# Weight preparation in a fused depthwise and pointwise convolution: copies as four concurrent 32-row matmuls, and the weight rows loaded by parity

## The chip, the cores and the metric

The kernel runs on one core of a Trainium2 chip. The metric is the time of one execution on the device in microseconds (us). Medians are given with the lowest and highest run. A profile is one execution; its "span" runs from the first to the last instruction, and is some 1.7 us shorter than the time of the same execution.

## The reference

A depthwise convolution with a 1x1 kernel is a scaling of each channel; a pointwise one is a matrix product. With H = W = C = D = 384 and bf16 throughout:

```python
def reference(x, dw, pw):            # x (1,384,384,384), dw (1,1,384), pw (384,384)
    out = x * dw[0, 0]               # k = 1: no padding, no sum over taps
    return jnp.einsum('bhwc,cd->bhwd', out, pw)
```

The kernel folds dw into pw, w[c, d] = dw[c] * pw[c, d], and multiplies 147456 pixels by w.

## The kernel before

Pixels are worked through in 288 "supertiles" of 512. VectorE transposes 32x32 blocks of channel pairs (bf16 pairs as one 32-bit word), so the channels of a 64-channel block b stand as pairs on 32 partitions. A matmul then takes the even or the odd channel of each pair (`par`), 32 rows deep, four of them side by side on the four 32-row strips of the array:

```python
mm = nc.tensor.matmul(PS[s][:, q, :D],                      # the main loop, 48 per supertile
        lhsT=Ts[s][32*q : 32*q+32, b, par::2],
        rhs=w_r[32*q : 32*q+32, b, par, :],
        tile_position=(32*q, 0), ...)
```

Each strip q needs the same 32 weight rows of (b, par), so w_r holds every row four times over the partitions. That is prepared once, in the "head", ahead of the loop. pw is loaded in natural order, 128 rows outermost. A 0/1 selector, scaled by dw, picks 32 rows and copies them to four strips in one 128-row matmul; ScalarE and VectorE then move the result out of PSUM:

```python
nc.sync.dma_start(pw_n[:, 0, :], pw[:P, :]).then_inc(s_pw[0], 16)
nc.sync.dma_start(pw_n[:, 1:3, :], pw[P:, :].rearrange("(k p) d -> p k d", p=P)).then_inc(s_pw[1], 16)
# ... TensorE:
idle_work(4)                          # rounds of four matmuls of zeros
# dw on partitions: 3 matmuls of 128 columns;  then idle_work(2)
for b in range(NB):                   # NB = 6
    # ... waits for pw, the scaled selector, PSUM banks that are free again
    for r in range(2):
        mm = nc.tensor.matmul(w_ps(b)[:, r, :], lhsT=sel_w[:, b//2, 2*(b%2)+r, :],
                              rhs=pw_n[:, b//2, :], start=True, stop=True)
    mm.then_inc(s_w)
# six evictions of 128x768: number 1 on VectorE, the other five on ScalarE
```

## Time and profile before

| | before |
|---|---|
| time, median of 6 (lowest to highest) | 576.05 us (575.57 to 578.58) |
| span of the profiled run | 573.9 us |
| first main matmul | 7.40 us |
| 288 supertiles | 561.8 us, 1.951 us each |
| after the start of the last group of matmuls | 5.1 us |

TensorE sets the time. From 7.40 us it never waits, so the time is the head, plus 288 x 1.951 us, plus the last eviction and store. The prediction shows the lines. A group of four concurrent matmuls of 384 columns takes 0.1625 us in the loop, and twice as long, 0.32 us, while the array runs at half rate. In the lines of the profile, PE is TensorE's matmuls and PEld its weight loads, DVE is VectorE, ACT ScalarE, POOL GpSimd and SP SyncE; a q behind the name stands for the queue that issues that engine's DMAs, L is a line of the kernel, and x with a number is a count.

### The profile page before, as it was taken

Reading aid. Unit: us, or ns where it says so; the run is one execution under the profiler, and the core shown is the slowest. Engines: PE = TensorE matmul, PEld = TensorE weight load, DVE = VectorE, ACT = ScalarE, POOL = GpSimd, SP = SyncE. Lnnn points to the kernel's source line nnn. Section 1 sums busy time; section 2 is a strip of 40 time slices with the busy share of each in tenths; the row PEclk is TensorE's granted clock in tenths of the full one; section 3 lists DMA queues with packets and bytes.
Section 4 is the critical chain, followed back from the end, with each engine's and each line's share of the span. In section 5 each row is a group of like instructions: output and inputs, shape, how many; then the busy total and the mean of one; then the engine's idle time right before and its main releaser. Section 6 shows DMA issues by size and latency. Waiting matters only on the chain.

```text
span 573.9 us, 29696 instructions
## 1 busy us (share of the span) xinstructions
PE 567.2 (99%) x13863; PEld 412.2 (72%) x13863; DVE 506.9 (88%) x582; ACT 418.9 (73%) x296; POOL 1.7 (0%) x8
## 2 busy tenths in 40 slices
PE   8999999999999999999999999999999999999996
PEld 4777777777777777777777777777777777777774
DVE  6898988988898898889889988988998898899884
ACT  6777777777777777777777777777777777777775
POOL 1000000000000000000000000000000000000000
PEclk9999999999999999999999999999999999999999
DMA  8999999999999999999999999999999999994996
GB/s 339 432 391 427 421 418 426 435 429 417 382 405 420 385 392 436 392 390 397 434 391 385 398 434 383 400 400 432 399 387 422 407 384 398 422 392 156 410 404 244
DMA packets 25928, 226.88 MB, mean 395 GB/s; under 512 B 1213, under 2 KB 5694, under 8 KB 22078
## 3 DMA queue, kind: packets, MB, share of 16 engines
q1 hardware_dynamic: 25916, 226.79, 98.1%
q14 instruction: 9, 0.07, 0.0%
q8 instruction: 1, 0.02, 0.0%
q10 hardware_dynamic: 2, 0.00, 0.0%
HBM read 113.54 MB, written 113.25 MB: 395 GB/s over the span
## 4 chain that ended last, share of the span: by engine, by line
PE 98%; ACT 1%; DMA 0%; DVE 0%; issue 0%; POOL 0%; POOLq 0%; SPq 0%
PE ps L165 97%; PE ps L182 0%; DMA out_dram<-O 0%; PE ps L214 0%; ACT w_r L268 0%; ACT O L296 0%; DVE O L293 0%; POOL zero L229 0%; POOL warm L228 0%; PE ps L197 0%; POOLq L326 0%; SPq L99 0%
## 5 line engine op out<-in xcount | busy, mean ns | idle before, releaser
L165 PE MATMUL ps<-w_r,T 32*128 32x384 bf16 x13824 | 561.8, 321 | 0.5 <-ACT w_r L268 0.5
L255 DVE STREAM_TRANSPOSE T<-X 128x384 uint32<-128x384 uint32 x576 | 504.0, 878 | 55.9 <-DMA X<-in_x_dram 1.2
L296 ACT CAST O<-ps 128x1536 bf16<-128x1536 f32 x288 | 413.6, 1436 | 147.7 <-PE ps L165 147.7
L165 PEld LDWEIGHTS ps<-w_r,T 32*128 32x128 bf16 x13824 | 410.2, 93 | 152.0 <-issue 0.8
L268 ACT CAST w_r<-ps 128x768 bf16<-128x768 f32 x5 | 3.7, 810 | 1.9 <-PE ps L214 1.8
L182 PE MATMUL ps<-zero 32*128 32x384 bf16 x24 | 2.6, 494 | 1.4 <-POOL zero L229 1.4
L293 DVE CAST O<-ps 128x768 bf16<-128x768 f32 x1 | 1.0, 957 | 3.0 <-DMA out_dram<-O 3.0
L273 DVE COPY dw_f<-ps 128x3 f32<-128x3 f32 x1 | 0.2, 160 | 3.3 <-PE ps L197 3.3
L214 PE MATMUL ps<-pw_n,sel_w 128*128 128x384 bf16 x12 | 2.8, 382 | 0.1
L182 PEld LDWEIGHTS ps<-zero 32*128 32x128 bf16 x24 | 0.7, 99 | 2.6 <-issue 2.6
L214 PEld LDWEIGHTS ps<-pw_n,sel_w 128*128 128x128 bf16 x12 | 1.2, 111 | 1.8 <-issue 0.9
L241 ACT ACT_TABLE_LOAD x1 | 1.3, 1283 | 1.5 <-SPq L99 1.5
L268 DVE CAST w_r<-ps 128x768 bf16<-128x768 f32 x1 | 1.0, 958 | 1.0 <-PE ps L214 1.0
L277 DVE TENSOR_SCALAR sel_w<-sel,dw_f 128x512 bf16<-128x512 bf16 x3 | 0.9, 348 | 0.1
L231 POOL TENSOR_SCALAR_AFFINE_SELECT sel<-ones 128x512 bf16<-128x512 bf16 x1 | 0.7, 735 | 0.1
L230 POOL MEMSET ones<- 128x512 bf16 x1 | 0.5, 529 | 0.0
L197 PEld LDWEIGHTS ps<-ones,dw_row 1*128 1x128 bf16 x3 | 0.2, 98 | 0.2 <-issue 0.2
L241 ACT COPY warm<-warm 128x1 f32<-128x1 f32 x2 | 0.3, 189 | 0.0
L229 POOL MEMSET zero<- 128x192 uint32 x1 | 0.3, 258 | 0.0
L197 PE MATMUL ps<-ones,dw_row 1*128 1x1 bf16 x3 | 0.2, 160 | 0.0
L228 POOL MEMSET warm<- 128x3 f32 x1 | 0.1, 101 | 0.5 <-SPq L99 0.5
L315 POOL MEMSET const-bfloat16-1.0<- 128x1 bf16 x1 | 0.1, 101 | 0.0
(3 smaller groups left out, 0.3 us busy)
## 6 DMA issues: line engine op xcount, KB each, us to landing
X<-in_x_dram SPq DMA_DIRECT2D x26, 3840.0 KB, 21.5
out_dram<-O SPq DMA_DIRECT2D x26, 3840.0 KB, 27.4
X<-in_x_dram SPq DMA_DIRECT2D x2, 1536.0 KB, 17.3
out_dram<-O SPq DMA_DIRECT2D x2, 1536.0 KB, 13.3
X<-in_x_dram SPq DMA_DIRECT2D x3, 768.0 KB, 7.5
out_dram<-O SPq DMA_DIRECT2D x3, 768.0 KB, 11.1
X<-in_x_dram SPq DMA_DIRECT2D x1, 2304.0 KB, 19.0
out_dram<-O SPq DMA_DIRECT2D x1, 2304.0 KB, 11.8
```

What stands on the lines that cost most here:

```text
L165: mm = nc.tensor.matmul(PS[s][:, q, :D], lhsT=Ts[s][32 * q : 32 * q + 32, b, par::2], rhs=w_r[32 * q : 32 * q + 32, b, par, :], start=(b = ...
L182: nc.tensor.matmul(PS[0][:, i, :D], lhsT=zero[32 * i : 32 * i + 32, 0:P], rhs=zero[32 * i : 32 * i + 32, :], start=True, stop=True, tile_p ...
L197: mm = nc.tensor.matmul(PS[1][:, k, D : D + 1], lhsT=dw_row[:, P * k : P * k + P], rhs=ones[0:1, 0, 0:1], start=True, stop=True,)
L214: mm = nc.tensor.matmul(w_ps(b)[:, r, :], lhsT=sel_w[:, b // 2, 2 * (b % 2) + r, :], rhs=pw_n[:, b // 2, :], start=True, stop=True,)
L230: nc.gpsimd.memset(ones[:], 1.0).then_inc(s_seed)
L231: nc.gpsimd.affine_select(out=sel[:].rearrange("p (v r) (q w) -> p v r q w", v=2, q=4), in_=ones[:].rearrange("p (v r) (q w) -> p v r q w" ...
L241: c = nc.scalar.copy(warm[:, s + 1 : s + 2], warm[:, 0:1])
L255: ins = nc.vector.transpose(out=Tw[:, 3 * h : 3 * h + 3], in_=Xw[:, :, j, 96 * h : 96 * h + 96].rearrange("p k (b w) -> p b k w", w=32),)
L268: i = nc.vector.tensor_copy(out, in_) if e == 0 else nc.scalar.copy(out, in_)
L277: nc.vector.tensor_scalar_mul(sel_w[:, k], sel[:], dw_f[:, k : k + 1]).then_inc(s_sw)
L293: e = nc.vector.tensor_copy(Ov[:, nq:4, j, :], PS[s][:, nq:4, :D])
L296: a = nc.scalar.copy(Ov[:, 0:nq, j, :], PS[s][:, 0:nq, :D])
```

## The change

The intent is a shorter head. Four weight copies run side by side on the four strips, with one 32-column selector in place of four 128-column ones. Each strip must then hold 32 rows of the same parity, so the load permutes the rows of pw: within each third (128 rows), even rows to partitions 0 to 63, odd ones to 64 to 127. dw is spread by twelve 32-column matmuls, and two idle rounds are dropped. Cut to its core:

```diff
-        nc.sync.dma_start(pw_n[:, 0, :], pw[:P, :]).then_inc(s_pw[0], 16)
-        nc.sync.dma_start(pw_n[:, 1:3, :], pw[P:, :].rearrange("(k p) d -> p k d", p=P)).then_inc(s_pw[1], 16)
+        for k, eng in enumerate((nc.sync, nc.sync, nc.scalar)):
+            rows = pw[P * k : P * k + P, :].rearrange("(u r) d -> r u d", r=2)
+            eng.dma_start(pw_n[:, k, :], rows).then_inc(s_pw[k], 16)
 # [cut: main loop, last four groups in the order (4,0) (5,0) (4,1) (5,1)]
-        idle_work(4)
+        idle_work(3)
 # [cut: dw by twelve matmuls of 32 columns instead of three of 128]
-        idle_work(2)
-        for b in range(NB):
+        idle_work(1)
+        for k in range(3):
 # [cut: waits for pw third k, selector k, and for k == 2 the first two evictions]
+            for j in range(4):
                 mm = nc.tensor.matmul(
-                    w_ps(b)[:, r, :],
-                    lhsT=sel_w[:, b // 2, 2 * (b % 2) + r, :],
-                    rhs=pw_n[:, b // 2, :],
+                    PS[(k + 1) % 2][:, j, :D],
+                    lhsT=sel_w[32 * j : 32 * j + 32, k, :, :].rearrange("p q w -> p (q w)"),
+                    rhs=pw_n[32 * j : 32 * j + 32, k, :],
+                    tile_position=(32 * j, 0),
 # [cut: selector from a 128x128 unit matrix by a VectorE reduction; evictions by parity]
```

More of the change, by code (lines that the diff above doesn't have):

```diff
@@ L67 @@
     pw_n = consts.tile([P, 3, D], BF16, name="pw_n")
-    ones = consts.tile([P, 4, P], BF16, name="ones")
-    sel = consts.tile([P, 4, P], BF16, name="sel")
-    sel_w = consts.tile([P, 3, 4, P], BF16, name="sel_w")
+    ones = consts.tile([P, P], BF16, name="ones")
+    eye = consts.tile([P, P], BF16, name="eye")
+    sel = consts.tile([P, 32], F32, name="sel")
+    sel_w = consts.tile([P, 3, 4, 32], BF16, name="sel_w")
     w_r = consts.tile([P, NB, 2, D], BF16, name="w_r")
@@ L88 @@
     s_dw = nc.alloc_semaphore("s_dw")
-    s_pw = [nc.alloc_semaphore(f"s_pw{h}") for h in range(2)]
+    s_pw = [nc.alloc_semaphore(f"s_pw{h}") for h in range(3)]
     s_df = nc.alloc_semaphore("s_df")
@@ L147 @@
         w_eng = [1, 0, 1, 1, 1, 1]
-        w_done = [(s_wr[e], w_eng[: b + 1].count(e)) for b, e in enumerate(w_eng)]
-        w_first = {0: [(0, 1), (1, 3)], 4: [(1, 4)], 5: [(1, 5)]}
-        def w_ps(b):
-            return PS[0 if b in (2, 3) else 1][:, 2 * (b % 2) : 2 * (b % 2) + 2, :D]
-        def supertile(s, rv):
-            for b in range(NB):
-                for par in range(2):
-                    for q in range(4):
-                        if par == 0 and q == 0 and b in (0, 3):
-                            nc.tensor.wait_ge(s_t[s][b // 3], rv)
-                        if s == 0 and par == 0 and q == 0 and b in w_first:
-                            for e, v in w_first[b]:
-                                nc.tensor.wait_ge(s_wr[e], v)
-                        mm = nc.tensor.matmul(
-                            PS[s][:, q, :D],
-                            lhsT=Ts[s][32 * q : 32 * q + 32, b, par::2],
-                            rhs=w_r[32 * q : 32 * q + 32, b, par, :],
-                            start=(b == 0 and par == 0),
-                            stop=(b == NB - 1 and par == 1),
-                            tile_position=(32 * q, 0),
-                        )
-                        if b == 0 and par == 0 and q == 0:
-                            mm._wait_ge(s_a[s], rv)
-                        if b in (2, 5) and par == 1 and q == 3:
-                            mm.then_inc(s_pe)
@@ new lines, with w_ps @@
+        w_done = [(s_wr[e], w_eng[: i + 1].count(e)) for i, e in enumerate(w_eng)]
+        w_first = {(0, 0): [(0, 1), (1, 3)], (4, 0): [(1, 4)], (4, 1): [(1, 5)]}
+        def w_ps(i):
+            return PS[0 if i in (2, 3) else 1][:, 2 * (i % 2) : 2 * (i % 2) + 2, :D]
+        steps = [(b, par) for b in range(4) for par in range(2)] + [(4, 0), (5, 0), (4, 1), (5, 1)]
+        def supertile(s, rv):
+            for b, par in steps:
+                for q in range(4):
+                    if q == 0 and par == 0 and b in (0, 3):
+                        nc.tensor.wait_ge(s_t[s][b // 3], rv)
+                    if q == 0 and s == 0:
+                        for e, v in w_first.get((b, par), []):
+                            nc.tensor.wait_ge(s_wr[e], v)
+                    mm = nc.tensor.matmul(
+                        PS[s][:, q, :D],
+                        lhsT=Ts[s][32 * q : 32 * q + 32, b, par::2],
+                        rhs=w_r[32 * q : 32 * q + 32, b, par, :],
+                        start=(b, par) == steps[0],
+                        stop=(b, par) == steps[-1],
+                        tile_position=(32 * q, 0),
+                    )
+                    if (b, par) == steps[0] and q == 0:
+                        mm._wait_ge(s_a[s], rv)
+                    if (b, par) in ((2, 1), (5, 1)) and q == 3:
+                        mm.then_inc(s_pe)
@@ L191 @@
         nc.tensor.wait_ge(s_zero, 1)
-        idle_work(4)
+        idle_work(3)
+        nc.tensor.wait_ge(s_seed, 2)
         nc.tensor.wait_ge(s_dw, 16)
-        nc.tensor.wait_ge(s_seed, 2)
         for k in range(3):
-            mm = nc.tensor.matmul(
-                PS[1][:, k, D : D + 1],
-                lhsT=dw_row[:, P * k : P * k + P],
-                rhs=ones[0:1, 0, 0:1],
-                start=True,
-                stop=True,
-            )
-        mm.then_inc(s_df)
-        idle_work(2)
-        for b in range(NB):
-            if b in (0, 2):
-                nc.tensor.wait_ge(s_pw[b // 2], 16)
-            if b % 2 == 0:
-                nc.tensor.wait_ge(s_sw, b // 2 + 1)
-            if b >= 4:
-                nc.tensor.wait_ge(*w_done[b - 4])
-            for r in range(2):
+            for j in range(4):
+                r0 = P * k + 64 * (j % 2) + j // 2
                 mm = nc.tensor.matmul(
-                    w_ps(b)[:, r, :],
-                    lhsT=sel_w[:, b // 2, 2 * (b % 2) + r, :],
-                    rhs=pw_n[:, b // 2, :],
+                    PS[1][32 * j : 32 * j + 32, 0, D + k : D + k + 1],
+                    lhsT=dw_row[:, r0 : r0 + 63 : 2],
+                    rhs=ones[0:1, 0:1],
                     start=True,
                     stop=True,
+                    tile_position=(0, 32 * j),
+                )
+        mm.then_inc(s_df)
+        idle_work(1)
+        for k in range(3):
+            nc.tensor.wait_ge(s_pw[k], 16)
+            nc.tensor.wait_ge(s_sw, k + 1)
+            if k == 2:
+                nc.tensor.wait_ge(*w_done[0])
+                nc.tensor.wait_ge(*w_done[1])
+            for j in range(4):
+                mm = nc.tensor.matmul(
+                    PS[(k + 1) % 2][:, j, :D],
+                    lhsT=sel_w[32 * j : 32 * j + 32, k, :, :].rearrange("p q w -> p (q w)"),
+                    rhs=pw_n[32 * j : 32 * j + 32, k, :],
+                    start=True,
+                    stop=True,
+                    tile_position=(32 * j, 0),
                 )
@@ L231 @@
         nc.gpsimd.affine_select(
-            out=sel[:].rearrange("p (v r) (q w) -> p v r q w", v=2, q=4),
-            in_=ones[:].rearrange("p (v r) (q w) -> p v r q w", v=2, q=4),
-            pattern=[[-64, 2], [-1, 2], [0, 4], [-2, 32]],
+            out=eye[:],
+            in_=ones[:],
+            pattern=[[-1, P]],
             compare_op=mybir.AluOpType.is_equal,
@@ L263, with w_out @@
         order = [(t, j) for t in range(NT) for j in range(chunks[t][4])]
-        def w_out(b):
-            e = w_eng[b]
-            out, in_ = w_r[:, b, :, :], w_ps(b)
-            i = nc.vector.tensor_copy(out, in_) if e == 0 else nc.scalar.copy(out, in_)
-            i._wait_ge(s_w, b + 1)
-            i.then_inc(s_wr[e])
+        def w_out(i):
+            e, k, r = w_eng[i], i // 2, i % 2
+            out, in_ = w_r[:, 2 * k : 2 * k + 2, r, :], w_ps(i)
+            o = nc.vector.tensor_copy(out, in_) if e == 0 else nc.scalar.copy(out, in_)
+            o._wait_ge(s_w, k + 1)
+            o.then_inc(s_wr[e])
+        nc.vector.wait_ge(s_sel, 1)
+        nc.vector.tensor_reduce(
+            out=sel[:],
+            in_=eye[:].rearrange("p (q w) -> p w q", q=4),
+            op=mybir.AluOpType.add,
+            axis=mybir.AxisListType.X,
+        ).then_inc(s_dwf)
         nc.vector.wait_ge(s_df, 1)
-        nc.vector.tensor_copy(dw_f[:].rearrange("p (k o) -> p k o", o=1), PS[1][:, 0:3, D : D + 1]).then_inc(s_dwf)
-        nc.vector.wait_ge(s_sel, 1)
-        nc.vector.wait_ge(s_dwf, 1)
+        nc.vector.tensor_copy(dw_f[:], PS[1][:, 0, D : D + 3]).then_inc(s_dwf)
+        nc.vector.wait_ge(s_dwf, 2)
         for k in range(3):
-            nc.vector.tensor_scalar_mul(sel_w[:, k], sel[:], dw_f[:, k : k + 1]).then_inc(s_sw)
-        for b in range(NB):
-            w_out(b)
+            nc.vector.tensor_scalar_mul(
+                sel_w[:, k], sel[:].unsqueeze(1).to_broadcast([P, 4, 32]), dw_f[:, k : k + 1]
+            ).then_inc(s_sw)
+        for i in range(6):
+            w_out(i)
         transposes(*order[0])
```

## The prediction

> **What bounds the kernel now.** I read the page's busy times and its chain of waits first, to see which engine sets the end and from when; then the chain in order of time, which says how much of the span lies ahead of the steady loop, where alone the change acts; then the first 8 us instruction by instruction, and the list of waits.
>
> ```profile
> span 573.9 us, 29696 instructions
> PE 567.2 (99%) x13863; PEld 412.2 (72%) x13863; DVE 506.9 (88%) x582; ACT 418.9 (73%) x296; POOL 1.7 (0%) x8
> ...
> L165 PE MATMUL ps<-w_r,T 32*128 32x384 bf16 x13824 | 561.8, 321 | 0.5 <-ACT w_r L268 0.5
> ```
>
> The main matmuls (L165) start once and never idle again: 0.5 us is all the idle time before them, and it lies ahead of the first. 288 supertiles in 561.8 us are 1.951 us each; a supertile is 12 groups of four concurrent matmuls, so a group takes 162.5 ns. The diff reorders the last four groups of a supertile but leaves their number, size and buffers, so this term stays.
>
> ```profile
> 1.43 1.74 PE ps L182 x14
> 3.16 0.06 PE ps L197 x3
> 3.23 0.79 PE ps L182 x8
> 4.02 0.02 issue
> 4.04 1.70 PE ps L214 x6
> 5.73 0.02 issue
> 5.76 1.51 ACT w_r L268 x2
> 7.26 0.14 issue
> 7.40 557.90 PE ps L165 x13728
> 565.31 0.02 issue
> ```
>
> This is the chain in order of time (start, length, what). The loop starts at 7.40 us. What follows 569.2 us (last eviction, last store, 4.7 us together) is not touched. So the question is by how much 7.40 moves. Ahead of it stand four rounds of idle matmuls, the three matmuls for dw (L197), two more idle rounds, the weight copies (L214), and three ScalarE copies of 128x768 out of PSUM (0.80 us each, 0.69 us apart when back to back), of which the third, ending at 7.26, lets the loop begin.
>
> ```profile
> 3.54 0.35 DVE L277 TENSOR_SCALAR sel_w<-sel,dw_f 128x512 bf16<-128x512 bf16 x1
> 4.31 0.84 PE L214 MATMUL ps<-pw_n,sel_w 128*128 128x384 bf16 x2
> 5.56 0.65 PE L214 MATMUL ps<-pw_n,sel_w 128*128 128x384 bf16 x3
> 25.35 2.28 DVE L255 STREAM_TRANSPOSE T<-X 128x384 uint32<-128x384 uint32 x3 [1.24 <-DMA X<-in_x_dram]
> ```
>
> These are from the timeline. The first scaled selector is ready at 3.89, but the first weight copy starts at 4.04: the idle matmuls, not the selector, set that start. Two copies from 4.31 take 0.84 us, of which one alone takes 0.52, so they start 0.32 us apart; the three from 5.56 start 0.16 us apart (0.65 less 0.33, halved). TensorE's rate doubled at about 5.2 us. The last line is the single place where a transpose waits for input: supertile 10, the first of the first ten-supertile load.
>
> **What the Trainium skill says.** "TensorE: Matmul & The Clock Gate", Part 1 (the HAM clock gate), has the array at half rate until it was busy through a window of about 3.4 us; the window runs freely, so the moment varies between runs. The trace agrees: 384 columns 0.32 us apart, then 0.16, 3.8 us after the first matmul. Part 3 (packing small matmuls) lets matmuls on different 32-row strips run together. The trace agrees: 162.5 ns for four, the time of one. "TensorEngine Tiling (Array Packing)", Key Properties, says that a change of tiling mode drains the array; the trace shows next to nothing for it, since from the first L197 weight load (2.98) to the next idle one (3.09) three load-and-multiply pairs take 0.11 us. "DMA: Bandwidth & Descriptors", the two cost components of one DMA, gives about 2 us of fixed time; the first pw load, issued at 1.01, landed 2.0 us later.
>
> **The change part by part.**
> *Idle work.* One idle round fewer ahead of dw. Rounds start 0.38 to 0.44 us apart, so L197 can start at 2.98 - 0.38 = 2.60, if dw is there. Its landing is not recorded. Its 768 bytes moved at 1.8 to 1.9, and for pw the landing came about 0.4 us after its last bytes, so about 2.3 is likely; 2 us after the issue at 0.97 would be 2.97. The second idle block also loses a round.
> *dw.* Three matmuls of 128 columns become twelve of 32. At 0.11/3 = 37 ns a pair, nine more add 0.33 us, and I choose 0.05 for mode changes. VectorE's copy of dw started 0.28 after the first L197 load: so 2.60 + 0.28 + 0.38 = 3.26, just where it is now. The early start pays for the longer fan.
> *Selector.* GpSimd's memset (0.53) and select (0.73) shrink to a quarter of the elements; the new VectorE reduction reads 128 elements, surely under 0.4 us. All ends before 2.5, beside the wait for dw: nothing. The scaling writes 128 elements instead of 512 but reads float32; I choose 0.30 instead of 0.35. So selector 0 is ready at 3.26 + 0.28 + 0.30 = 3.84.
> *First weight matmul.* The remaining idle round ends near 3.6 and pw landed at 3.0, so it starts at 3.88 instead of 4.04: 0.16 us won. pw's split into three loads, one on the other issuing queue, brings the second third no later than today's 4.0, and it is needed about 0.3 us after the first.
> *Copies.* Today ScalarE's first copy starts 0.83 us after the first weight matmul (two in sequence, 0.27 + 0.52, and a signal); its second waits for matmuls (5.76 instead of 5.56, 0.20 lost). Four concurrent ones take the 0.51 us that a cold idle round shows, plus 0.04: 0.55, so 0.28 less. The second group follows 0.33 us later, before ScalarE is free, so the 0.20 goes too. In all 0.48 us. Check: 3.88 + 0.55 + two steps of 0.69 + 0.81 + 0.14 = 6.76, against 7.40: 0.64 us. PSUM evictions keep their number and size; reading by parity changes only addresses.
> *Last two copies.* They must be through before the second supertile, and before groups 9 and 11 of the first. As now, they are early enough.
> The sum is -0.64 us, a tenth of a per cent.
>
> **The rivals.**
> 1. *A new wait for x.* The transpose of supertile 10 ends at 25.35 + 0.88 = 26.23, and TensorE needs it at 7.40 + 10 x 1.951 = 26.91. The margin is 0.68 us. An earlier start uses it up: beyond 0.68 nothing can be won, and if that load lands 0.2 us later (the DMA engines are full up to then and stores come earlier), 0.2 of the 0.64 is lost in a TensorE gap near 26 us. This makes 575.4 into 575.6. Against it: no further wait for x exists, and later slack is never called on.
> 2. *dw lands late.* If it lands at 2.97, the longer fan is on the path: 3.36 + 0.28 = 3.64 instead of 3.26, first weight matmul at 4.26, loop at 7.14, gain 0.26: 575.8. For it: today's L197 starts at just 2.98. Against it: that is also when a row strip of the last idle round comes free (2.65 + 0.33).
> 3. *The clock stays slow.* The new head does less matmul work: 16 idle matmuls instead of 24, waits for dw, and about 0.8 us idle before the loop. If the rate then doubles not at 5.2 but a window later, near 8.6, the loop runs at half rate from 6.76 to 8.6 and loses half of it, 0.9 us: net +0.3, 576.35. For it: today TensorE was busy almost throughout 1.43 to 5.2; afterwards I estimate some 75%. Against it: gaps stay far under a window.
> 4. *The fan is much dearer*, say 100 ns a pair: 0.6 us more, gain gone: 576.05.
>
> **Range and chances.** The best case is -0.64, with rival 1 about -0.5; I give these together 55%, rival 2 25%, and rivals 3 and 4 20% (+0.15 on average). Weighted: 0.55 x -0.55 + 0.25 x -0.26 + 0.20 x 0.15 = -0.34, and I round towards the likeliest case: -0.45 from 576.05 gives 575.6. The three runs before spread by 0.6 us, as large as the effect, and another session can shift both; so the range is 574.9 to 576.5. Faster or slower by 2% would be 11.5 us. The head before the loop is 7.4 us in all, so faster is impossible short of an error of mine; slower would need a stall in the loop. Chances: 0.003 faster, 0.99 within 2%, 0.007 slower.
>
> **What would show it.** Right, if: the first L165 starts between 6.6 and 7.2 us; L214 shows groups of four within about 0.1 us; the first two evictions (ScalarE and VectorE) start together, about 0.55 us after the first weight matmul; scaling takes about 0.3 us; a supertile stays 1.951 us. Rival 1 shows as TensorE idle time before L165, released by a transpose, near 26 us; rival 2 as L197 starting at or after 2.98; rival 3 as main matmul groups 0.32 us apart after the start; rival 4 in the spacing of L197. The prediction is wrong if the loop's term moves at all: then I have overlooked what the new order of groups does.

## The result and the profile after

| | before | after |
|---|---|---|
| time, median of 6 | 576.05 us | 584.75 us (583.81 to 585.38) |
| span of the profiled run | 573.9 us | 582.1 us |
| first main matmul | 7.40 us | 14.26 us |

The ratio is 1.0146 (95% interval 1.0126 to 1.0166). Ratios here are the mean time of one kernel's fast runs over that of the other's fast runs of the same rounds, so they are not quite the ratios of the medians. The change made the kernel 1.5% slower. That is within 2%, but 8.25 us above the top of the predicted range.

The page of the changed kernel (groups: line, engine, operation; then busy time in us and mean ns of one; then idle time before them and what ended it). The main matmuls are now L168, the weight copies L219:

```profile
span 582.1 us, 29696 instructions
...
L168 PE MATMUL ps<-w_r,T 32*128 32x384 bf16 x13824 | 563.1, 321 | 1.4 <-ACT w_r L274 1.4
...
L219 PE MATMUL ps<-pw_n,sel_w 32*128 32x384 bf16 x12 | 1.3, 504 | 8.2 <-DMA pw_n<-in_pw_dram 8.2
```

The weight copies themselves shrank, from 2.8 us busy to 1.3, but TensorE now waits 8.2 us for the loads of pw. The chain of waits in order of time (start, length, what) says the same:

```profile
1.01 0.70 SPq L134
...
1.77 10.24 DMA pw_n<-in_pw_dram
...
12.06 0.53 PE ps L219 x4
...
12.62 1.51 ACT w_r L274 x2
...
14.26 559.19 PE ps L168 x13243
```

Where the idle rounds and weight copies stood on the path before, there now stands one load of 96 KB that takes 10.24 us from its issue. The DMA issues of the first microseconds (number, KB each, median us to landing where the profile has it), the kernel before first, then the one after:

```profile
X<-in_x_dram SPq DMA_DIRECT2D x2, 384.0 KB, 3.9
pw_n<-in_pw_dram SPq DMA_DIRECT2D x1, 192.0 KB, 2.5
pw_n<-in_pw_dram SPq DMA_DIRECT2D x1, 96.0 KB, 2.0
```

```profile
X<-in_x_dram SPq DMA_DIRECT2D x2, 384.0 KB, 10.5
...
pw_n<-in_pw_dram SPq DMA_DIRECT2D x2, 96.0 KB
pw_n<-in_pw_dram ACTq DMA_DIRECT2D x1, 96.0 KB
```

The landing column is empty for pw, and x's first tiles, whose loads are the same as before, land late too. Both have one reason, and it shows in the records of the semaphores. A completed load adds 16 to its semaphore. These are the times in us at which it was updated (for before the first, the last and their number):

```
before, first load of pw   : 2.65 ... 3.02         (16 updates)
before, second load of pw  : 3.56 ... 3.98         (16 updates)
after, third 0 of pw       : 2.10, 6.26, 6.53      (3 updates)
after, third 1 of pw       : 2.94, 11.62, 12.02    (3 updates)
after, third 2 of pw       : 2.58, 9.90, 10.13     (3 updates)
after, first tile of x     : 5.95 ... 6.51, then 12.52 and 12.86  (14 + 2)
```

The Trainium skill explains this pattern in "DMA: Bandwidth & Descriptors", in the section on why a DMA increments its semaphore by 16 and not by 1. A DMA issued by SyncE or ScalarE is split over the largest number k of engines, up to 16, that divides the slowest dimension of both access patterns; the issuer writes the other 16 - k increments at once, and each engine adds 1 when its part has landed. `"(u r) d -> r u d"` with r = 2 makes 2 the slowest dimension, so k = 2. The trace agrees: one early update and two late ones. Each of the two engines then carries 64 of the 128 rows of each third, 192 rows in all, where sixteen engines carried 24 each before. The 384 row packets of 768 bytes start between 2.03 and 3.63 us before, and between 2.46 and 11.23 us after: 8.8 us / 192 = 46 ns a row on average. x's tiles are spread over all sixteen, but two of their sixteenths queue behind pw. That would by itself have held the loop almost as long: the transpose of x's first tile ended at 13.76 us, the third ScalarE copy, for which the loop waited, at 14.13.

That accounts for 14.26 - 7.40 = 6.86 of the 8.2 us in the trace. The rest is at the start of the loop. Busy time by engine in stretches of 1 us, with the number of instructions in brackets, first the kernel before, then the one after:

```profile
core 0: us, PE busy (x) PEld busy (x) DVE busy (x) ACT busy (x) POOL busy (x), PEclk, DMA share, GB/s
...
8.00:9.00 1.00, 1.00 (x32) 0.72 (x26) 1.00 (x2) 0.66 (x1) 0.00 (x0) 1.00 1.04 436
```

```profile
15.00:16.00 1.00, 1.00 (x20) 0.56 (x16) 0.81 (x2) 0.53 (x1) 0.00 (x0) 1.00 1.38 584
16.00:17.00 1.00, 1.00 (x20) 0.53 (x12) 0.58 (x1) 0.00 (x0) 0.00 (x0) 1.00 1.09 467
17.00:18.00 1.00, 1.00 (x32) 0.67 (x25) 0.57 (x2) 0.28 (x1) 0.00 (x0) 1.00 1.04 449
```

TensorE is busy in all of these, but from 15 to 17 us it has only 20 matmuls in a microsecond under way where there are 32 otherwise. The first nine steps from group to group are up to 0.32 us apart, and together they cost 1.28 us more than at 0.1625. The column PEclk stays at 1.00; it does not show this half rate. TensorE had waited from about 7.1 to 12.06 us. So 6.86 + 1.28 = 8.14 of 8.2 us are accounted for, and the loop itself, with its new order of groups, is as fast as before: 0.162 or 0.163 us from group to group from there to the end.

### The profile page after: what moved, and what is told of

Read it like the earlier page. It is cut to its first block, busy times and chain, and to the rows that moved or that the text cites. A ratio compares the mean times of both kernels' runs of the same rounds, so it can differ in the third digit from the quotient of the medians.

```text
span 582.1 us, 29696 instructions
## 1 busy us (share of the span) xinstructions
PE 566.4 (97%) x13864; PEld 380.0 (65%) x13864; DVE 507.8 (87%) x583; ACT 419.1 (72%) x296; POOL 0.9 (0%) x8
## 4 chain that ended last, share of the span: by engine, by line
PE 96%; DMA 2%; ACT 1%; DVE 0%; SPq 0%; issue 0%
PE ps L168 96%; DMA pw_n<-in_pw_dram 2%; DMA out_dram<-O 0%; ACT w_r L274 0%; ACT O L310 0%; DVE O L307 0%; SPq L134 0%; PE ps L219 0%; SPq L340 0%; SPq L100 0%
## 5 line engine op out<-in xcount | busy, mean ns | idle before, releaser
L168 PE MATMUL ps<-w_r,T 32*128 32x384 bf16 x13824 | 563.1, 321 | 1.4 <-ACT w_r L274 1.4
L168 PEld LDWEIGHTS ps<-w_r,T 32*128 32x128 bf16 x13824 | 379.0, 93 | 185.6 <-issue 1.8
L219 PE MATMUL ps<-pw_n,sel_w 32*128 32x384 bf16 x12 | 1.3, 504 | 8.2 <-DMA pw_n<-in_pw_dram 8.2
L219 PEld LDWEIGHTS ps<-pw_n,sel_w 32*128 32x128 bf16 x12 | 0.4, 99 | 9.0 <-DMA pw_n<-in_pw_dram 9.0
```

Of the source, the lines that this page charges most:

```text
L168: mm = nc.tensor.matmul(PS[s][:, q, :D], lhsT=Ts[s][32 * q : 32 * q + 32, b, par::2], rhs=w_r[32 * q : 32 * q + 32, b, par, :], start=(b, ...
L219: mm = nc.tensor.matmul(PS[(k + 1) % 2][:, j, :D], lhsT=sel_w[32 * j : 32 * j + 32, k, :, :].rearrange("p q w -> p (q w)"), rhs=pw_n[32 * ...
```

## The experiments

The theory is in two parts. First, the load with a slowest dimension of 2 runs on two engines, and that alone makes the loop late. Second, with less matmul work in the head the array is at half rate when the loop starts. The rivals: reading every second row is slow in itself (1); three loads on two queues collide with x (2); the new matmuls and copies cost the time (3). For each run the profile gives the start of the loop and what the loop loses in slow groups or gaps. These add up to the change in the span, so the first four columns can be checked against the last:

| run | time, median us | loop starts | lost in the loop | sum against before | span against before |
|---|---|---|---|---|---|
| after | 584.75 | 14.26 | 1.28 | +8.14 | +8.2 |
| a_natural | 577.03 | 7.11 | 2.13 | +1.84 | +1.9 |
| a_halves | 579.67 | 8.68 | 2.68 | +3.96 | +5.6 |
| a_first_spread | 582.36 | 12.28 | 1.79 | +6.67 | +6.7 |
| b_load | 583.52 | 14.60 | 0.20 | +7.40 | +7.4 |
| a_filler | 582.63 | 13.84 | 0.00 | +6.44 | +6.5 |
| b_less_idle | 576.29 | 7.06 | 0.00 | -0.34 | +0.5 |
| pairs | 577.88 | 6.95 | 1.64 | +1.19 | +1.2 |
| pairs_fill | 577.27 | 6.87 | 1.44 | +0.91 | +1.1 |
| pairs_busy | 575.80 | 7.18 | 0.14 | -0.08 | +2.4 |
| pairs_2 | 576.73 | 6.93 | 1.53 | +1.06 | +1.1 |
| pairs_busy_2 | 575.40 | 6.75 | 0.43 | -0.22 | -0.2 |

Four rows differ by over 0.1 in the last two columns: a_halves, b_less_idle, pairs_fill and pairs_busy. In the profiles of these the time from the last group of matmuls to the end is 6.7, 5.9, 5.3 and 7.5 us; in all others it is 5.1. The last store ends later there; why was not looked into. The kernel before, in the rounds of these experiments, had a median of 576.03 to 576.27 us and single runs up to 579.19.

**a_natural: the changed kernel with pw in natural row order** (wrong result: the rows are not where the selector expects them).

```diff
-            rows = pw[P * k : P * k + P, :].rearrange("(u r) d -> r u d", r=2)
-            eng.dma_start(pw_n[:, k, :], rows).then_inc(s_pw[k], 16)
+            eng.dma_start(pw_n[:, k, :], pw[P * k : P * k + P, :]).then_inc(s_pw[k], 16)
```

> The changed kernel with its three pw loads in natural row order (128 rows outermost) on the same queues; the result is wrong on purpose. Theory (the load with a size-2 outermost dimension runs on two DMA engines only): each load completes in 16 steps again, pw lands near 3.0 to 3.7 us, the loop starts near 6.4, 575.0 to 575.6 us. Rival 1 (reading every second row is slow in itself): also 575. Rival 2 (three loads, one on the second queue, collide with x): stays near 584. Rival 3 (the new matmuls and copies cost the time): stays near 584.

577.03 us (576.58 to 577.48), ratio 1.0006 (0.9989 to 1.0024). All three loads complete in 16 updates, the last at 3.98 us. From its timeline:

```profile
3.65 0.83 PE L218 MATMUL ps<-pw_n,sel_w 32*128 32x384 bf16 x8 [0.25 <-DVE sel_w L288]
4.21 3.61 ACT L273 CAST w_r<-ps 128x768 bf16<-128x768 f32 x5 [0.72 <-PE ps L218]
6.15 2.93 DVE L260 STREAM_TRANSPOSE T<-X 128x384 uint32<-128x384 uint32 x4 [0.98 <-DMA X<-in_x_dram]
7.11 4.35 PE L167 MATMUL ps<-w_r,T 32*128 32x384 bf16 x52 [1.29 <-ACT w_r L273]
```

With the same number of loads on the same queues, and the same matmuls and evictions, 7.7 of the 8.7 us of the medians are gone. That rules out rivals 2 and 3 as the main cause. The expected 575.0 to 575.6 was missed all the same. The first tile of x landed whole only at 6.13 us, and its transpose ended at 7.01, so the loop started at 7.11 and not 6.4. (The last line names a ScalarE copy as what ended the wait, because the fourth one ends at 7.12. The kernel asks for three of them before the first group, and the third was done at 6.42; with the 0.14 us from a copy to the first matmul, the loop could have started near 6.56 but for x.) And 14 steps at or near half rate cost 2.13 us.

**b_load: the kernel before with the loads of the changed kernel** and nothing else (wrong result).

```diff
-        nc.sync.dma_start(pw_n[:, 0, :], pw[:P, :]).then_inc(s_pw[0], 16)
-        nc.sync.dma_start(pw_n[:, 1:3, :], pw[P:, :].rearrange("(k p) d -> p k d", p=P)).then_inc(s_pw[1], 16)
+        for k, eng in enumerate((nc.sync, nc.sync, nc.scalar)):
+            rows = pw[P * k : P * k + P, :].rearrange("(u r) d -> r u d", r=2)
+            eng.dma_start(pw_n[:, k, :], rows).then_inc(s_pw[k], 16)
```

> The kernel before with nothing changed but its pw loads, which are those of the changed kernel; the result is wrong on purpose. Theory: three completion steps per load, the second third lands near 12, the loop starts near 14.5, 583 to 585 us. Rival 3 (the matmuls and copies): 576.

583.52 us (583.04 to 584.76), ratio 1.0129 (1.0110 to 1.0147), with three updates for each load:

```profile
1.77 10.11 DMA pw_n<-in_pw_dram
11.88 0.05 issue
11.93 2.74 PE ps L215 x8
14.67 558.03 PE ps L166 x10295
```

The load alone makes the old kernel about as slow as the new one. It loses only 0.20 us in slow groups: its serial 128-row copies keep TensorE at work for 2.7 us just before the loop.

**a_first_spread: only the first third of pw as two loads of 64 rows.**

```diff
+            if k == 0:
+                for r in range(2):
+                    eng.dma_start(pw_n[64 * r : 64 * r + 64, k, :], rows[r]).then_inc(s_pw[k], 16)
+            else:
-            eng.dma_start(pw_n[:, k, :], rows).then_inc(s_pw[k], 16)
+                eng.dma_start(pw_n[:, k, :], rows).then_inc(s_pw[k], 16)
# and TensorE waits for 32 instead of 16 on the first third
```

> The changed kernel with only the first third of pw loaded as two 64-row halves; the second and third stay with the size-2 outermost dimension. Theory: the first third lands near 3.2, the two engines have 128 packets of pw instead of 192, so the second third lands near 8.5 instead of 12.0, the loop starts near 10.7 with a slow clock for a while, 579 to 581.5 us. Rival 1: the halves are as slow as before and the loop does not start earlier, 584.

582.36 us (581.36 to 582.83). The direction is right and the size was off. The first half landed at 3.21, so rows two apart are not slow in themselves (rival 1). Of the second half, 14 parts landed by 4.05 and the last two at 6.65 and 6.87; those two engines also carried the third on the second queue, which completed at 7.21. Third 1 landed at 10.03, not at 8.5. The number of rows was nearly right: a busy engine has 4 + 4 + 64 + 64 = 136, where the expectation said 128. At 46 ns a row the last would start at 8.7 us, 6.3 after the first at 2.40; the trace has it at 9.24, 50 ns a row. The landing came another 0.8 us later, as in the changed kernel (11.23 and 12.02), so 8.5 was nearer to the start of the last row than to its landing.

**a_halves: pw in two loads of 64 rows by all three thirds, one on each queue.**

```diff
-        for k, eng in enumerate((nc.sync, nc.sync, nc.scalar)):
-            rows = pw[P * k : P * k + P, :].rearrange("(u r) d -> r u d", r=2)
-            eng.dma_start(pw_n[:, k, :], rows).then_inc(s_pw[k], 16)
+        for r, eng in enumerate((nc.sync, nc.scalar)):
+            rows = pw.rearrange("(k u r) d -> r u k d", k=3, r=2)[r]
+            eng.dma_start(pw_n[64 * r : 64 * r + 64, :, :], rows).then_inc(s_pw[r], 16)
```

> The changed kernel with pw loaded by two DMAs, one for even and one for odd rows, 64 rows outermost, all three thirds in each; the result is right. Theory: every engine takes part, pw lands before 3.2 us, the loop starts near 6.4, 575.0 to 575.6 us, with up to 0.3 us of wait near supertile 10. Rival 1 (every second row is slow): loop after 10 us, 580 to 584. Rival 3: near 584.

579.67 us (577.85 to 581.24), correct. It is 5 us better than the change, but a miss. The half on the second queue completed between 4.14 and 4.66 us on fifteen engines and at 5.69 on the last, so the loop started at 8.68, and then lost 2.68 us at half rate. The permuted rows with 64 outermost do spread over 16 engines; why that one engine lagged stays open.

**a_filler: the changed kernel with 20 rounds of idle matmuls after the first weight group.** The loads are untouched.

```diff
             mm.then_inc(s_w)
+            if k == 0:
+                for n in range(20):
+                    for i in range(4):   # 32-row matmuls of zeros into PS[0][:, i, :D]
+                        nc.tensor.matmul(...)
```

> The changed kernel with 20 rounds of idle matmuls between the first weight group and the wait for the second third of pw, so that TensorE is busy while it waits; loads untouched, result right. Theory (of 8.2 us lost in the trace, 6.9 are the late load and 1.28 are eight groups at half rate because TensorE idled): the loop still starts near 14.3 but its groups are 0.16 us apart from the first, 583.3 to 583.7 us. Rival (the slow groups come from something else, as the fresh w_r or x): slow groups stay, 584.75.

582.63 us (582.11 to 583.05), 2.1 us below the change without it. The first full stretch of its loop:

```profile
14.00:15.00 1.00, 1.00 (x32) 0.74 (x28) 1.00 (x3) 1.00 (x2) 0.00 (x0) 1.00 1.01 412
```

There are 32 matmuls from the start and not one slow group. The spans differ by 1.7 us: the 1.28 us, and 0.42 by which the loop starts earlier (13.84 against 14.26), of which 0.27 are an earlier landing of the second third (11.75 against 12.02). The expected 583.3 to 583.7 us was thus too high, but work that computes nothing, done while TensorE would have waited, saves the 1.28 us: the second part of the theory holds.

**b_less_idle: the kernel before with one idle round instead of six.**

```diff
-        idle_work(4)
+        idle_work(1)
# ...
-        idle_work(2)
```

> The kernel before with one idle round instead of six, nothing else. Theory: the loop starts no later (6.5 to 7.4), but the head's matmul work no longer brings the rate up by then: slow groups (0.32 us) for 1 to 4 us after the start, 576.3 to 578.5 us. Rival (the head's work is not what decides the rate): no slow groups, 575.2 to 576.1.

576.29 us (576.08 to 577.14), ratio 0.9996 (0.9971 to 1.0021). The expected slow groups did not come in the profiled run:

```profile
3.30 3.64 PE ps L213 x12
6.94 0.12 issue
7.06 557.90 PE ps L165 x13728
```

The twelve serial copies, 3.64 us without a pause, were enough in this run. They start 0.32 us apart up to 6.45 us and only the last two 0.16 apart, so the full rate came 0.6 us before the loop. The idle rounds were not needed here: the slow weight copies gave TensorE work enough. That rests on one profile.

**pairs: pw loaded in pairs of neighbouring rows.** It is a repaired form of the change. Partition p gets rows 2p and 2p+1 as 1536 contiguous bytes (128 partitions, then 64), so parity is a choice of columns and the load permutes nothing:

```diff
+        nc.sync.dma_start(pw_n[:, 0], pw[: 2 * P, :].rearrange("(p r) d -> p (r d)", r=2)).then_inc(s_pw[0], 16)
+        nc.sync.dma_start(pw_n[:64, 1], pw[2 * P :, :].rearrange("(p r) d -> p (r d)", r=2)).then_inc(s_pw[1], 16)
# weight groups: blocks 0-3 even, blocks 0-3 odd, then blocks 4 and 5; dw by four matmuls
```

> The changed kernel with pw loaded as pairs of neighbouring rows (1536 bytes to a partition, 128 partitions, then 64): no permutation of rows in the load, 16 engines, half the packets; parity becomes the choice of a column block. Weight groups: blocks 0 to 3 even rows, then odd, then blocks 4 and 5. Result right. Theory: both loads land before 4 us, the loop starts at 6.4 to 6.7 (x's first tile lands near 5.5), at a slow clock for 1 to 5 us, so 576.0 to 578.0. If the clock theory is wrong: 575.0 to 575.4.

577.88 us (576.81 to 579.55), ratio 1.0024 (1.0003 to 1.0045), correct. The loads land by 3.46 and 4.60 us and the loop starts at 6.95. The first tile of x landed last at 5.97, and then 1.64 us are lost in eleven slow steps.

**pairs_fill: the same with the second weight group issued twice and the third three times.**

```diff
-            for n in range(1):
+            for n in range((1, 2, 3)[m]):
                 for j in range(4):
```

> As the paired kernel, with the second weight group issued twice and the third three times (same values into the same banks), so that TensorE idles less before the loop. Theory: the loop starts at 6.4 to 6.8 and in most runs at full rate or with few slow groups, 575.2 to 576.2, below the paired kernel by up to 1.5 us; if 85% busy is still too little for the clock, the same as the paired kernel.

577.27 us (576.75 to 579.23). The loop starts at 6.87 and the half rate stays: 1.44 us are lost, partly under repeated copies that still run beside the loop's first groups. So much filling was too little.

**pairs_busy: the gaps filled with 128-row matmuls of zeros**, eleven in all. The last five add zero to a bank that is read later, so that values stay right.

```diff
-        idle_work(3)
+        filler(PS[0][:, 3, :D], 3, True)     # and again after dw, instead of idle_work(1)
# ... after each weight group m:
             mm.then_inc(s_w)
+            if m == 1:
+                filler(PS[0][:, 3, :D], 3, False).then_inc(s_w)
+            elif m == 2:
+                filler(PS[1][:, 3, :D], 2, False).then_inc(s_w)
```

> The paired kernel with its gaps ahead of the loop filled by 128-row matmuls of zeros: three before dw, three before the first weight group, three after the second group and two after the third, the last five adding zero to a bank that is read later, so that values stay right. TensorE then streams almost without a gap from 1.43 us to the loop. Theory (what the repaired change lacks is matmul work in the head): the loop starts at 6.4 to 7.0 with no or few slow groups in most runs, 575.0 to 576.2 us, one to two us below the paired kernel. If fillers don't help: 577 to 578 with about ten slow groups, and the clock's cause stays open.

575.80 us (575.28 to 577.98), ratio 0.9982 (0.9959 to 1.0005), correct. It was timed once more, beside the plain form on one chip:

> The paired kernel again, beside its filled form on one chip, because the two were timed on different occasions. Theory: 577 to 578.5 us with some ten slow groups after the start of the loop, 1 to 2.5 us slower than the filled form.

> The filled form again. Theory: no or few slow groups, 575.3 to 576.2 us; against the kernel before a ratio of 0.998 to 1.000, too near 1 to be called faster, since its loop starts only about 0.2 us earlier (7.18 against 7.40) and runs differ by up to 2 us through the last store.

576.73 us (576.36 to 577.43) without the filling, a little under the expected 577, and 575.40 us (575.09 to 576.50) with it. The loop's second microsecond in pairs_2, then in pairs_busy_2:

```profile
8.00:9.00 1.00, 1.00 (x20) 0.57 (x15) 0.90 (x2) 0.00 (x0) 0.00 (x0) 1.00 1.00 406
```

```profile
8.00:9.00 1.00, 1.00 (x32) 0.71 (x25) 0.64 (x1) 0.08 (x2) 0.00 (x0) 1.00 0.95 332
```

20 matmuls against 32, and 1.3 us in the medians. Both parts of the theory are thus shown on a correct kernel: with the load spread and TensorE at work through the head, the change's idea costs no time. But it hardly gains anything either. The two ratios of the filled form to the kernel before are 0.9982 (0.9959 to 1.0005) and 0.9993 (0.9979 to 1.0007); it can't be called faster. One reason shows in the timeline of pairs_busy_2:

```profile
10.11 2.27 DVE L265 STREAM_TRANSPOSE T<-X 128x384 uint32<-128x384 uint32 x3 [1.47 <-DMA X<-in_x_dram]
...
11.07 1.16 PE L167 MATMUL ps<-w_r,T 32*128 32x384 bf16 x24 [0.24 <-issue]
```

Its loop starts at 6.75, 0.65 us before that of the kernel before. The transpose of supertile 2 then waits 1.47 us for the third load of x, and the step between two groups around 10.5 to 11.1 us is 0.59 us instead of 0.16. Of the 0.65 us, 0.43 are given back.

## Why the prediction was wrong

- **The step that failed** is in "First weight matmul": "pw's split into three loads, one on the other issuing queue, brings the second third no later than today's 4.0". I counted the loads and their bytes and took the reordering of rows for a matter of addresses. It landed at 12.02 instead. The slowest dimension of the pattern is 2, two engines carry 192 rows each at 46 ns, and the wait for pw put the start of the loop at 14.26 instead of the predicted 6.76 us, 6.86 later than before the change. b_load shows this alone, and a_natural shows the change without it. None of the four rivals was about the loads of pw: I asked what might take the place of the wait that goes, but not what the new access pattern does to the transfer. The rule for the number of engines stands in the Trainium skill, in the section cited above, and the prediction did not use it.
- **Rival 3, the slow clock, came true** and I gave it too little. "Gaps stay far under a window" was wrong in the changed kernel (5 us), and without the late load the half rate still cost 1.5 to 2.1 us (a_natural, pairs, pairs_2). I had counted fewer idle rounds; b_less_idle shows that those were not needed. What is missing is the matmul time that the concurrent copies save: in the profiles, 3.64 us in series brought the array to full rate (b_less_idle), three short groups did not (a_natural, pairs, pairs_2).
- **dw and the selector** were better than I chose. dw's last update comes at 2.17 us in the trace of the kernel before, so it had landed and rival 2 is out. The twelve matmuls took 0.25 us, so rival 4 is out. One scaling took 0.28 us (0.30 chosen), the reduction 0.37 (under 0.4). The first scaled selector was ready at 3.49, not 3.84. "Its landing is not recorded" was wrong: the semaphore's updates had it.
- **The copies** were right: the first two evictions start together, 0.56 us after their matmuls (0.55 predicted), here in the timeline of the changed kernel:

```profile
2.71 0.25 PE L202 MATMUL ps<-ones,dw_row 1*32 1x1 bf16 x12
6.57 0.51 PE L219 MATMUL ps<-pw_n,sel_w 32*128 32x384 bf16 x4 [3.18 <-DMA pw_n<-in_pw_dram]
7.13 0.80 ACT L274 CAST w_r<-ps 128x768 bf16<-128x768 f32 x1 [3.36 <-PE ps L219]
7.13 0.96 DVE L274 CAST w_r<-ps 128x768 bf16<-128x768 f32 x1 [3.24 <-PE ps L219]
```

- **The loop's term** was right: the reordered groups cost nothing.
- **Rival 1, a new wait for x**, is real but lies elsewhere: at the loop's first transpose (a_natural and pairs start when x's first tile is transposed) and at supertile 2 (pairs_busy_2). None showed at supertile 10, but no run came there early enough to test it. So even the best case of -0.64 us was not to be had in full.
- **Within 2%** was right, as a class, for a wrong reason: the prediction's bound on a slowdown ("slower would need a stall in the loop") overlooked that a head can grow.
- **What stays open:** how much of a window must be busy for the full rate, since few doses of filling were tried, pairs_fill and pairs_busy differ in the kind of matmul as well as in the amount, and each run has one profile; why one engine lagged in a_halves; and why some runs end with a last store 0.2 to 2.4 us later.

## What to carry to other kernels

When a change touches how a load is written, work out the slowest dimension of both access patterns before anything else, and count the updates of its semaphore in the trace: one early and two late ones mean two engines, and everything queued behind them waits too. Work that looks slow can be what keeps the TensorE rate up; before it is removed, ask how busy the array will be in the last microseconds ahead of the loop, and compare the number of matmuls per microsecond, since neither busy share nor granted clock shows the half rate. A gain that is smaller than the spread of the runs needs its mechanism read from the trace, term by term, and a clear look at the next wait behind it.

## What the Trainium skill lacked or had wrong

- "DMA: Bandwidth & Descriptors", the two cost components of one DMA: the page's fit, about 2 us plus bytes over bandwidth, is for DMAs that GpSimd issues. Used as an estimate for these loads, which SyncE issues, it would give 2.2 us for 98304 bytes. That is near only where the load is spread: 2.0 us with 16 engines, 10.24 us from issue for the second third with two. The rule for the number of engines stands in another section, without the price: 41 to 50 ns a row of 768 bytes on an engine, taken over the runs with this load (46 in the changed kernel, 41 in a_filler, 50 in a_first_spread), and x's first tile delayed from 6.51 us (14 parts) to 12.86 (the last two) behind it.
- "TensorE: Matmul & The Clock Gate", Part 1: it speaks of a busy window of about 3.4 us but not of how busy it must be. Here 3.64 us of unbroken serial matmuls ahead of the loop sufficed in the profiled run (b_less_idle); the rate doubled some 3.1 us after the first of them. A head with four idle rounds and three short groups left eleven slow steps in pairs and ten in pairs_2, and a head with filled gaps (pairs_busy_2) left none.
- "TensorEngine Tiling (Array Packing)", Key Properties: a change of mode is said to drain the array, without a figure. In pairs_busy the last 128-row matmul before a weight group starts at 3.38 and streams for 0.32 us, and the first 32-row weights are loaded at 3.84, with selector and pw there since 3.48: some 0.14 us. The three later changes between 128 and 32 rows in that head show 0.13 to 0.14 us too. This is a gap that stands at each change; that all of it is the drain is not shown. It is not the "next to nothing" that the prediction read from the dw matmuls, which are one row deep and stand between 32-row ones, so they say nothing of a change to 128 rows.
